# A decode block on one core: x as columns, w_o in fewer pieces, the residual matmul behind w_up, the output in one row

## The chip, the cores and the metric

The kernel runs on one core of a Trainium2 chip. The metric is the device time of one execution in microseconds (us); of several runs the median is given. Beside it stands the *span*, the time from the first to the last instruction of the kernel itself, as the hardware profiler gives it. The time is in most runs 1.8 to 2.1 us longer than the span: the trace shows semaphores being cleared after the kernel's last instruction (their last update 1.91 us after it in the trace of the kernel before).

Names: PE is the tensor engine (PEld its weight load), DVE the vector engine, ACT the scalar engine, POOL the general engine, SP the engine that issues most DMAs (SPq, ACTq: a DMA issue by SP or ACT). A DMA has *landed* when the last of its semaphore updates has come (16 for each large load).

## The reference, cut to what matters

One token goes through attention over a cache of 65536 keys and values for 8 heads of 128 columns each, four query heads per cache head, and through a gated MLP:

```
h  = x + attention(layernorm(x)) @ w_o          # x: 512 values
h2 = h + (sigmoid(n @ w_gate) * (n @ w_up)) @ w_down     # n = layernorm(h), 1792 inner columns
```

The caches have 268 MB; with the weights 282 MB must be read once. Everything else is small.

## The kernel before

All large loads are queued by SP in one order: w_q, the K and V blocks of 4 MiB each (32 of either), w_o, the last V blocks, w_gate, w_up, w_down. They go to a ring of four slots (w_o to `ktw`, the buffer of the transposed keys), and a load waits only until its place is free. The last loads are cut into pieces, so that work can begin on the first piece:

```python
WO = ((0, 16), (16, 8), (24, 4), (28, 4))          # w_o by heads: 4 pieces
WD_SPLIT = [(0, 7), (7, 12), (12, 14)]             # w_down by rows of 512
V_SPLIT = [(0, 3), (3, 4)]                         # last V block, in two pieces of two runs each
...
dma("act", lambda e: e.dma_start(x_row[:, :], A_x[0]), "x", name="x")       # one row of 512
...
for kt in range(4):                                # x into columns, by PE
    op("pe", lambda e, ...: e.matmul(ps(MISC, kt, kt + 1), lhsT=lhsT, rhs=ident[0:1, 0:1], ...), ...)
```

The tail of the program: the last heads' values, w_o, the norm, then gate, residual, up, down and the output.

```python
for i, (nm, bank) in enumerate((("wg", GB), ("wu", UB))):
    for kt in range(4):
        for c in range(4):
            op("pe", ... matmul(ps(bank, 0, FG, 32 * c, 32 * c + 1), lhsT=hc[:, kt:kt + 1], rhs=ring[...]) ...)
    if i == 0:                                     # residual h, between gate and up
        op("pe", lambda e: e.matmul(ps(YB, 0, 128), lhsT=gsel[:, :], rhs=hz[:, :], start=True, stop=False, ...), ["hz"])
op("act", ... sg = tanh(gate) ...)
op("dve", ... hh = up * sg2 ...)                   # then hhT: transpose of hh
for i, (r0, r1) in enumerate(WD_SPLIT):
    for r in range(r0, r1):
        for g in range(4):                         # four matmuls a row of w_down, on four column groups
            op("pe", ... matmul(ps(YB, 0, 128, 32 * g, 32 * g + 1), lhsT=hhT[...], rhs=wd_v[:, r, ...]) ...)
op("dve", lambda e: e.tensor_copy(y_sb[:, :], ps(YB, 0, 128)), ["y"], "ysb")
dma("sp", ... out as four rows of 128 from four partitions ...)
```

## Time and profile before

| | before |
|---|---|
| time, median of 6 runs | 661.88 us (661.62 to 662.31) |
| span of the profiled run | 659.8 us |
| read from memory | 282.3 MB, 428 GB/s over the span |
| PE, DVE, ACT busy | 64%, 53%, 6% |

The page of the profile begins with the busy time of each engine; below it the span is cut into 40 slices, with the granted TensorE clock (PEclk) and the busy share of the DMA engines in tenths:

```profile
span 659.8 us, 6128 instructions
...
PE 419.5 (64%) x2316; PEld 72.6 (11%) x1548; DVE 350.5 (53%) x446; ACT 41.8 (6%) x111; POOL 3.6 (1%) x17
...
PEclk9899687678888697776966778766878869678676
DMA  9999999999999999999999999999999999999997
...
DMA packets 11211, 282.34 MB, mean 428 GB/s; under 512 B 1225, under 2 KB 1226, under 8 KB 2250
```

The reader is to see the row of nines: the 16 DMA engines are at least 90% busy in every slice but the last, and the packets' records show no gap from 1.0 to 656.7 us. PE is busy 64% and DVE 53% of the time, and both wait for data: 160.2 of the 163.9 us that PE idles before the score matmuls end with DVE's transposed keys, and 137.4 of the 137.5 us that DVE idles before it transposes them end with a landing of K. So a microsecond saved on an engine in the middle should buy nothing; only the two ends can count, the start before the stream flows and what is left to do when it ends.

The start in the timeline (columns: start in us, duration, engine, line of the source, operation, tiles, count, and in brackets the idle time before it and what ended it):

```profile
0.80 0.51 ACTq L331 DMA_DIRECT2D x_row<-in_A_x_dram  x1
...
7.22 0.29 PE L421 MATMUL PS<-ident,x_row 1*128 1x1 bf16 x4 [7.22 <-DMA x_row<-in_A_x_dram]
...
12.69 8.78 PE L438 MATMUL PS<-ring,xz 128*8 x32
```

x arrives at 7.2 us and its norm is done before w_q has landed (12.2). The end of the timeline:

```profile
650.87 1.66 PE L816 MATMUL PS<-ring,hc 128*1 128x448 bf16 x16 [0.26 <-DVE hc L803]
...
652.46 0.80 PE L822 MATMUL PS<-hz,gsel 128*128 128x128 f32 x2
...
653.18 1.54 PE L816 MATMUL PS<-ring,hc 128*1 128x448 bf16 x16
...
654.78 0.91 DVE L828 TENSOR_TENSOR hh<-PS,sg 128x448 bf16<-128x448 f32 x1 [1.08 <-PE PS L816]
655.73 0.65 DVE L831 STREAM_TRANSPOSE hhT<-hh 128x448 bf16<-128x448 bf16 x1
...
656.43 1.05 PE L836 MATMUL PS<-ring,hhT 128*1 128x128 bf16 x56 [1.70 <-DVE hhT L831]
657.53 0.29 DVE L840 CAST y_sb<-PS 128x128 bf16<-128x128 f32 x1 [1.16 <-PE PS L836]
657.85 0.65 SPq L841 DMA_DIRECT2D out_dram<-y_sb  x1
```

L816 are gate and up, with the residual (L822) between them; L828 is hh, L831 its transpose, L836 w_down, L840 the copy of y, L841 the output. The last pieces of the chain of work that ended last (start, duration, what) are:

```profile
655.73 0.66 DVE hhT L831
...
656.43 1.08 PE PS L836 x56
...
657.53 0.29 DVE y_sb L840
```

By this view the chain is one of computing: transpose, w_down, copy. But the last piece of w_down had landed at 657.15, while the matmuls that need it began at 657.20. Chain and stream end together.

### The profile page before, as it was taken

To read this page: it belongs to the slowest core of one execution; us is meant where nothing else is said; L and a number is where in the kernel's file an instruction comes from. 1 tells how busy PE (TensorE), PEld (TensorE's weight loads), DVE (VectorE), ACT (ScalarE), POOL (GpSimd) and SP (SyncE) were. 2 spreads that over 40 slices of the span, in tenths; PEclk is the share of its full clock that TensorE was granted. 3 is DMA by queue.
4 is the path that set the end of the run, shared out by engine and by line. 5 is a ranking of instruction groups with operands and counts; after the bars stand their busy time and mean duration, and the time that the engine had idled before them with its cause. 6 is when DMAs were issued, how large, how long until landed. Compare 5 with 4: busy or idle time off the path is not lost. (4 is left out here: it accounts for less than half of the span.)

```text
span 659.8 us, 6128 instructions
## 1 busy us (share of the span) xinstructions
PE 419.5 (64%) x2316; PEld 72.6 (11%) x1548; DVE 350.5 (53%) x446; ACT 41.8 (6%) x111; POOL 3.6 (1%) x17
## 2 busy tenths in 40 slices
PE   3786587638666685566765485764856668565845
PEld 1100011001000010010100110001100101001222
DVE  3697755548436655336555374475743565553102
ACT  0100200020001100020000200002000200002000
POOL 1000000000000000000000000000000000000000
PEclk9899687678888697776966778766878869678676
DMA  9999999999999999999999999999999999999997
GB/s 397 429 445 419 439 429 429 443 417 443 425 433 441 417 445 419 439 429 429 443 417 443 429 429 441 417 445 423 435 429 429 443 419 441 429 429 419 439 418 329
DMA packets 11211, 282.34 MB, mean 428 GB/s; under 512 B 1225, under 2 KB 1226, under 8 KB 2250
## 3 DMA queue, kind: packets, MB, share of 16 engines
q1 hardware_dynamic: 11208, 282.33, 99.7%
q14 instruction: 1, 0.01, 0.0%
q10 hardware_dynamic: 2, 0.00, 0.0%
HBM read 282.33 MB, written 0.00 MB: 428 GB/s over the span
## 5 line engine op out<-in xcount | busy, mean ns | idle before, releaser
L438 PE MATMUL PS<-ktw 128*128 128x512 bf16 x1024 | 300.9, 442 | 163.9 <-DVE ktw L519 160.2
L519 DVE STREAM_TRANSPOSE ktw<-ring 128x1024 f32<-128x1024 f32 x256 | 291.7, 1206 | 137.5 <-DMA ring<-in_A_k_cache_dram 137.4
L438 PE MATMUL PS<-ring,PT_sb 128*32 x1024 | 82.8, 453 | 24.4 <-issue 16.2
L438 PEld LDWEIGHTS PS<-ktw 128*128 x256 | 27.1, 106 | 415.7 <-issue 261.5
L573 DVE STREAM_TRANSPOSE PT_sb<-P_sb 128x512 bf16<-128x512 bf16 x32 | 20.2, 684 | 53.2 <-PE PS L610 51.8
L559 ACT ACTIVATE negmax<-PS 128x1 f32<-128x1 f32 x8 | 1.4, 171 | 527.7 <-PE PS L557 527.7
L438 PEld LDWEIGHTS PS<-ring,PT_sb 128*32 x1024 | 25.3, 116 | 81.3 <-issue 76.8
L524 DVE TENSOR_REDUCE M_sb<-PS 128x1 f32<-128x512 f32 x32 | 19.9, 684 | 24.1 <-PE PS L438 24.1
L563 ACT ACTIVATE P_sb<-PS,negmax 128x512 bf16<-128x512 f32 x32 | 21.5, 685 | 0.3
L580 DVE TENSOR_REDUCE lsum<-PS 128x1 f32<-128x4 f32 x8 | 1.3, 163 | 30.5 <-PE PS L578 30.5
L550 PE MATMUL PS<-identf,gm 128*1 128x128 f32 x16 | 3.2, 286 | 16.9 <-DVE gm L548 16.9
L623 DVE TENSOR_TENSOR Lw<-O,blk_of 128x128 bf16<-128x128 bf16 x4 | 1.1, 282 | 21.7 <-ACT O L614 21.7
L607 ACT ACTIVATE po_sb<-PS,rl 128x512 bf16<-128x512 f32 x8 | 5.5, 687 | 54.4 <-PE PS L438 54.4
L438 PE MATMUL PS<-ring,xz 128*8 x32 | 8.8, 443 | 0.0
L485 DVE STREAM_TRANSPOSE qt<-qh 32x512 bf16<-32x512 bf16 x1 | 0.7, 699 | 11.9 <-ACT qh L482 11.9
L557 PE MATMUL PS<-one_f,gmrep 1*128 1x1 f32 x16 | 3.8, 306 | 5.0 <-DVE gmrep L554 5.0
L438 PE MATMUL PS<-ktw,O 128*1 x26 | 6.9, 431 | 0.0
L563 ACT ACTIVATION_READ_ACCUMULATOR P_sb<-PS,negmax 128x1 f32 x32 | 6.5, 203 | 0.0
L610 PE MATMUL PS<-sel_bf,po_sb 128*128 128x4 bf16 x32 | 2.0, 168 | 6.3 <-ACT po_sb L607 6.3
L500 ACT ACTIVATE PS<-zcol 128x512 f32<-128x512 bf16 x8 | 5.0, 622 | 0.0
L421 PE MATMUL PS<-ident,x_row 1*128 1x1 bf16 x4 | 0.3, 174 | 7.2 <-DMA x_row<-in_A_x_dram 7.2
L666 DVE TENSOR_TENSOR yr<-PS,x_row 1x512 f32<-1x512 f32 x1 | 0.7, 679 | 7.8 <-PE PS L664 7.8
(81 smaller groups left out, 69.4 us busy)
## 6 DMA issues: line engine op xcount, KB each, us to landing
ring<-in_A_k_cache_dram SPq DMA_DIRECT2D x32, 4096.0 KB, 29.6
ring<-in_A_v_cache_dram SPq DMA_DIRECT2D x31, 4096.0 KB, 27.5
ring<-in_A_wq_dram SPq DMA_DIRECT2D x1, 4096.0 KB, 12.2
ring<-in_A_v_cache_dram SPq DMA_DIRECT2D x1, 3072.0 KB, 13.1
ktw<-in_A_wo_dram SPq DMA_DIRECT2D x1, 2048.0 KB, 9.8
ring<-in_B_w_gate_dram SPq DMA_DIRECT2D x1, 1792.0 KB, 18.6
ring<-in_B_w_up_dram SPq DMA_DIRECT2D x1, 1344.0 KB, 21.2
ktw<-in_A_wo_dram SPq DMA_DIRECT2D x1, 1024.0 KB, 11.9
```

What stands on the lines that cost most here:

```text
L438: return e.add_instruction(mybir.InstMatmult(name=nc.get_next_instruction_name(), engine=mybir.EngineType.PE, ins=[rhs, lhsT], outs=[e.low ...
L500: op("act", lambda e: e.activation(ps(PO, 0, 512), bass.AP(tensor=zcol, offset=0, ap=[[1, 128], [0, 512]]), AF.Copy), ["zcol"] if h == 0 e ...
L519: op("dve", lambda e, d=dst, sr=src: e.transpose(d, sr), deps, f"T{b}.{c}", to="T")
L524: op("dve", lambda e, u=u: e.tensor_reduce(M_sb[:, u % 4:u % 4 + 1], ps(u % NS, 0, 512), AX.X, ALU.max), [f"S{b}.{NC - NR + k}"], f"mx{u}" ...
L550: op("pe", lambda e: e.matmul(ps(MISC, 0, 128, 0, 1), lhsT=gm[:, :], rhs=identf[:, :], start=True, stop=True), [f"gm{h}"], f"gmT{h}", to="Q")
L557: op("pe", lambda e: e.matmul(ps(MISC, 128, 129), lhsT=gmrep[0:1, :], rhs=one_f[0:1, 0:1], start=True, stop=True), [f"gmrep{h}"], f"neg{h}")
L559: op("act", lambda e: e.activation(negmax[:, k:k + 1], ps(MISC, 128, 129), AF.Copy, scale=-att_scale), [f"neg{h}"], f"negmax{h}")
L563: op("act", lambda e, b=b: e.activation(P_sb[:, (b % 4) * 512:(b % 4 + 1) * 512], ps(b % NS, 0, 512), AF.Exp, bias=negmax[:, k:k + 1], sca ...
L573: op("dve", lambda e, b=b: e.transpose(PT_sb[:, (b % 4) * 512:(b % 4 + 1) * 512], P_sb[:, (b % 4) * 512:(b % 4 + 1) * 512]), [f"E{b}", f"o ...
L580: op("dve", lambda e: e.tensor_reduce(lsum[:, :], ps(MISC, 132, 136), AX.X, ALU.add), [f"l{h}"], f"ls{h}", to="D")
L607: op("act", lambda e: e.activation(po_sb[:, :], ps(PO, 0, 512), AF.Copy, scale=rl[:, :]), [f"PV{NR * h + NR - 1}", f"rl{h}"], f"po{h}", to ...
L610: op("pe", lambda e, t=t: e.matmul(ps(OX, 0, 4), lhsT=po_sb[:, t * 128:(t + 1) * 128], rhs=sel_bf[:, 8 * t:8 * t + 8:2], start=(t == 0), s ...
```

## The change

Its intent is to trim the two ends: fewer and larger pieces, no transposing of x by PE, one matmul less between gate and up, one output row instead of four.

```diff
-    WO = ((0, 16), (16, 8), (24, 4), (28, 4))
-    WD_SPLIT = [(0, 7), (7, 12), (12, 14)]
+    WO = ((0, 28), (28, 4))
+    RW = 4
+    WD_SPLIT = [(0, 9), (9, 13), (13, 14)]
...
-        dma("act", lambda e: e.dma_start(x_row[:, :], A_x[0]), "x", name="x")
+        dma("act", lambda e: e.dma_start(x_col[:, :], A_x[0].rearrange("o (p k) -> (o p) k", k=4)), "x", name="x")
...      last V block: the order of K's and V's chunks changes so that each piece is one run
-                        d2, s2 = (ap.rearrange("p (h c) -> p h c", h=2)[:, :, c0 * CH:c1 * CH] for ap in (dst, src))
+                        d2, s2 = (ap[:, 2 * c0 * CH:2 * c1 * CH] for ap in (dst, src))
...      q: four transposes of x and an empty matmul go; ACT clears the sum
-        for kt in range(4):
-            lhsT = bass.AP(tensor=x_row, offset=kt, ap=[[D, 1], [4, 128]])
-            op("pe", lambda e, lhsT=lhsT, kt=kt: e.matmul(ps(MISC, kt, kt + 1), lhsT=lhsT, rhs=ident[0:1, 0:1], ...
-        ln_stats(0, ("xTp", (MISC, 0, 4)), 0, 0)
+        ln_stats(0, lambda e: e.tensor_copy(hT[0][:, :], x_col[:, :]), "x", 0, 0)
...      w_o: 28 heads are regrouped by seven small matmuls instead of three; x is added in the norm
-            op("dve", lambda e: e.tensor_tensor(yr[:, :], ps(YB, 0, D, 0, 1), x_row[:, :], ALU.add), ["yr"], "yrs")
+            op("dve", lambda e: e.tensor_copy(yr[:, :], ps(YB, 0, D, 0, 1)), ["yr"], "yrs")
...      the loop of the value matmuls computes its registers ahead of the last wait (one more branch)
-            if i == 0:
-                op("pe", lambda e: e.matmul(ps(YB, 0, 128), lhsT=gsel[:, :], rhs=hz[:, :], ...), ["hz"])
+        op("pe", lambda e: e.matmul(ps(YB, 0, 128), lhsT=gsel[:, :], rhs=hz[:, :], ...), ["hz"])
...
-        op("dve", lambda e: e.tensor_copy(y_sb[:, :], ps(YB, 0, 128)), ["y"], "ysb")
-        dma("sp", ... four rows of 128 ...)
+        for g in (0, 2, 1, 3):          # 0 and 1 by DVE, 2 and 3 by ACT, into one partition
+            ...  copy of ps(YB, 0, 128, 32 * g, 32 * g + 1) to y_sb[:, 128 * g:128 * g + 128]
+        dma("sp", lambda e: e.dma_start(out[0], y_sb[:, :]), "out", [f"ysb{g}" for g in range(4)], "out")
```

More of the change, by code (lines that the diff above doesn't have):

```diff
@@ L257, in bass_sequential_preLN__gqa_block_cached__glu_gated_glu__decode_kernel @@
         zcol = sb("zcol", [128, 1], bf16)
-        x_row = sb("x_row", [1, D], bf16)
+        x_col = sb("x_col", [128, 4], bf16)
         xz = sb("xz", [128, 4 * 16], bf16)
@@ L281, in bass_sequential_preLN__gqa_block_cached__glu_gated_glu__decode_kernel @@
         hhT = sb("hhT", [128, FG], bf16)
-        y_sb = sb("y_sb", [128, 128], bf16)
+        y_sb = sb("y_sb", [1, D], bf16)
         W0 = NKT * CH
         O3 = sb("O3", [128, NQ], bf16)
-        Lw = [sb(f"Lw{i}", [128, 128], bf16) for i in range(len(WO))]
-        row_of = {n: sb(f"row_of{n}", [128, n], bf16) for n in (16, 8, 4)}
-        blk_of = {n: sb(f"blk_of{n}", [128, 128 // n], bf16) for n in (16, 8, 4)}
+        Lw = [sb(f"Lw{i}", [128, n * DH // RW], bf16) for i, (_, n) in enumerate(WO)]
+        row_of = sb("row_of", [128, RW], bf16)
+        blk_of = sb("blk_of", [128, 128 // RW], bf16)
         head_of = sb("head_of", [128, 4], fp32)
@@ L387, in bass_sequential_preLN__gqa_block_cached__glu_gated_glu__decode_kernel, with ln_stats @@
                                           bass.AP(tensor=head_of, offset=0, ap=[[4, 128], [0, 16], [1, 4], [0, 2]])), ["head"], "lsel")
-        for n in (16, 8, 4):
-            op("dve", lambda e, n=n: e.tensor_reduce(row_of[n][:, :], identf[:, :].rearrange("p (c r) -> p r c", r=n), AX.X, ALU.max),
-               (), f"row{n}")
-            op("dve", lambda e, n=n: e.tensor_reduce(blk_of[n][:, :], identf[:, :].rearrange("p (c r) -> p c r", r=n), AX.X, ALU.max),
-               (), f"blk{n}")
+        op("dve", lambda e: e.tensor_reduce(row_of[:, :], identf[:, :].rearrange("p (c r) -> p r c", r=RW), AX.X, ALU.max), (), "row")
+        op("dve", lambda e: e.tensor_reduce(blk_of[:, :], identf[:, :].rearrange("p (c r) -> p c r", r=RW), AX.X, ALU.max), (), "blk")
         op("dve", lambda e: e.tensor_reduce(bass.AP(tensor=gsel, offset=0, ap=[[128, 128], [32, 4]]),
                                             identf[:, :].rearrange("p (s j) -> p s j", s=4), AX.X, ALU.add), ["gs0", "identf"], "gsel")
-        def ln_stats(i, src_dep, bank, c0):
-            op("dve", lambda e: e.tensor_copy(hT[i][:, :], ps(*src_dep[1])), [src_dep[0]], f"hT.{i}")
+        def ln_stats(i, fill, dep, bank, c0):
+            op("dve", fill, [dep], f"hT.{i}")
             op("dve", lambda e: e.tensor_tensor(sq[:, :], hT[i][:, :], hT[i][:, :], ALU.mult), [f"hT.{i}"], f"sq.{i}")
@@ L416, in ln_rstd @@
                f"rstd.{i}")
-        for kt in range(4):
-            lhsT = bass.AP(tensor=x_row, offset=kt, ap=[[D, 1], [4, 128]])
-            op("pe", lambda e, lhsT=lhsT, kt=kt: e.matmul(ps(MISC, kt, kt + 1), lhsT=lhsT, rhs=ident[0:1, 0:1], start=True, stop=True,
-                                                          skip_group_check=True),
-               ["x", "ident"] if kt == 0 else (), "xTp" if kt == 3 else None)
-        ln_stats(0, ("xTp", (MISC, 0, 4)), 0, 0)
+        ln_stats(0, lambda e: e.tensor_copy(hT[0][:, :], x_col[:, :]), "x", 0, 0)
         ln_rstd(0, 0, 0, 1.0)
@@ L461, in project_q @@
         def project_q(e):
-            def none(start, stop):
-                return e.matmul(ps(1, 0, 512, 0, 8), lhsT=qz[:, 0:8], rhs=qz[:, 0:512], start=start, stop=stop, skip_group_check=True)
-            none(True, False)
             e.reg_mov(reg(e, 0), addr_of(xz, 8 + 7))
@@ L478, in project_q @@
                     e.reg_alu(reg(e, 4 + kt), reg(e, 4 + kt), 1024, ALU.add)
-            return none(False, True)
-        op("pe", project_q, ["xz", "wq", "identf", "lsel", "onef", "sel", "gsel", "row4", "PTz", "qz0"], "q")
+            return e.matmul(ps(1, 0, 512, 0, 8), lhsT=qz[:, 0:8], rhs=qz[:, 0:512], start=False, stop=True, skip_group_check=True)
+        op("act", lambda e: e.activation(ps(1, 0, 512, 0, 8), bass.AP(tensor=zcol, offset=0, ap=[[1, 8], [0, 512]]), AF.Copy), ["zcol"], "zq")
+        op("pe", project_q, ["zq", "xz", "wq", "identf", "lsel", "onef", "sel", "gsel", "row", "PTz", "qz0"], "q")
         op("act", lambda e: e.activation(
@@ L513, in dve_block @@
                 n = b * NC + c
-                src = ring[:, s * SLOT + c * CH: s * SLOT + (c + 1) * CH].bitcast(fp32)
+                at = s * SLOT + (2 * (c % NR) + c // NR) * CH
+                src = ring[:, at:at + CH].bitcast(fp32)
                 dst = ktw[:, (n % NKT) * CH:(n % NKT + 1) * CH].bitcast(fp32)
@@ L588, in pv_regs @@
                         e.reg_alu(reg(e, i), R["p"], 2 * (128 * tq + half), ALU.add)
-                        e.reg_alu(reg(e, i + 4), R["v"], 2 * (half * NR * TC + 4 * tq) * 128, ALU.add)
+                        e.reg_alu(reg(e, i + 4), R["v"], 2 * (half * TC + 4 * tq) * 128, ALU.add)
         def pv(b):
@@ L616, in head_out @@
                 clear_out(h + 1)
-        YT, STB, GB, UB, YB, OT = 0, MISC, 2, 3, 5, (1, 2, 3, 1)
+        YT, STB, GB, UB, YB, OT = 0, MISC, 2, 3, 5, (1, 1)
         def regroup(i):
             j0, n = WO[i]
+            m = 128 // RW
             op("dve", lambda e: e.tensor_tensor(Lw[i][:, :].rearrange("p (j c) -> p j c", j=n),
-                                                bass.AP(tensor=O2, offset=j0, ap=[[NQ, 128], [1, n], [0, 128 // n]]),
-                                                bass.AP(tensor=blk_of[n], offset=0, ap=[[128 // n, 128], [0, n], [1, 128 // n]]), ALU.mult),
-               [f"o2.{(j0 + n) // GS - 1}", f"blk{n}"], f"Lw{i}")
-            op("pe", lambda e: e.matmul(ps(OT[i], 0, n), lhsT=Lw[i][:, :], rhs=row_of[n][:, :], start=True, stop=True),
-               [f"Lw{i}", f"PT{NB - 1}" if i == 0 else None], f"O3p{i}")
+                                                bass.AP(tensor=O2, offset=j0, ap=[[NQ, 128], [1, n], [0, m]]),
+                                                bass.AP(tensor=blk_of, offset=0, ap=[[m, 128], [0, n], [1, m]]), ALU.mult),
+               [f"o2.{(j0 + n) // GS - 1}", "blk"], f"Lw{i}")
+            for v in range(n // RW):
+                lhsT = bass.AP(tensor=Lw[i], offset=v, ap=[[n * m, 128], [n // RW, 128]])
+                op("pe", lambda e, v=v, lhsT=lhsT: e.matmul(ps(OT[i], RW * v, RW * v + RW), lhsT=lhsT, rhs=row_of[:, :], start=True,
+                                                            stop=True, skip_group_check=True),
+                   [f"Lw{i}", f"PT{NB - 1}" if i == 0 else None] if v == 0 else (), f"O3p{i}" if v == n // RW - 1 else None)
             op("dve", lambda e: e.tensor_copy(O3[:, j0:j0 + n], ps(OT[i], 0, n)), [f"O3p{i}"], f"O3.{i}")
@@ L640, in project7 @@
         def project7():
-            for i in range(3):
-                regroup(i)
-            waits = [d for i in range(3) for d in (f"O3.{i}", f"wo{i}")]
+            regroup(0)
+            waits = ["O3.0", "wo0"]
             def rows(e):
@@ L723, in pe_flow @@
             pv_regs(e)
+            goto("products", "sums")
             section("B")
             e.reg_alu(p, p, 2 * 512, ALU.add)
-            e.reg_alu(v, v, 2 * CH, ALU.add)
+            e.reg_alu(v, v, 2 * 2 * CH, ALU.add)
             e.reg_alu(m, m, -1, ALU.add)
@@ L731, in rest @@
             def rest():
-                section("VL")
+                pv_regs(e)
                 e.reg_mov(m, 1)
                 e.reg_mov(k, 0)
-            away("br_ne", k, 0, "rest", rest, "sums")
+                section("VL")
+            away("br_ne", k, 0, "rest", rest, "products")
             away("br_eq", w, w0 - 12, "outs", lambda: section("O"))
@@ L797, in bass_sequential_preLN__gqa_block_cached__glu_gated_glu__decode_kernel @@
         P.part = {}
-        regroup(3)
-        project(range(NQ - GS, NQ), O3, ["O3.3", "wo3"], last=True)
-        ln_stats(1, ("yT", (YT, 0, 4)), STB, 0)
+        regroup(1)
+        project(range(NQ - GS, NQ), O3, ["O3.1", "wo1"], last=True)
+        ln_stats(1, lambda e: e.tensor_tensor(hT[1][:, :], ps(YT, 0, 4), x_col[:, :], ALU.add), "yT", STB, 0)
         op("dve", lambda e: e.scalar_tensor_tensor(hc[:, :], ps(STB, 0, 1).to_broadcast([128, 4]), -1.0 / D, hT[1][:, :],
@@ L820, in bass_sequential_preLN__gqa_block_cached__glu_gated_glu__decode_kernel @@
                        ["hc"] * (kt == 0 and c == 0) + dep, f"gu{i}" if kt == 3 and c == 3 else None)
-            if i == 0:
-                op("pe", lambda e: e.matmul(ps(YB, 0, 128), lhsT=gsel[:, :], rhs=hz[:, :], start=True, stop=False, skip_group_check=True),
-                   ["hz"])
+        op("pe", lambda e: e.matmul(ps(YB, 0, 128), lhsT=gsel[:, :], rhs=hz[:, :], start=True, stop=False, skip_group_check=True), ["hz"])
         op("act", lambda e: e.activation(sg[:, :], ps(GB, 0, FG), AF.Tanh, scale=rstd[1][:, 0:1]), ["gu0", "rstd.1"], "sg")
@@ L839, in bass_sequential_preLN__gqa_block_cached__glu_gated_glu__decode_kernel @@
                        ["hhT", f"wd{i}"] if r == r0 and g == 0 else (), "y" if last else None)
-        op("dve", lambda e: e.tensor_copy(y_sb[:, :], ps(YB, 0, 128)), ["y"], "ysb")
-        dma("sp", lambda e: e.dma_start(out[0].rearrange("o (g n) -> (o g) n", g=4),
-                                        bass.AP(tensor=y_sb, offset=0, ap=[[32 * 128, 4], [1, 128]])), "out", ["ysb"], "out")
+        for g in (0, 2, 1, 3):
+            if g < 2:
+                op("dve", lambda e, g=g: e.tensor_copy(y_sb[:, 128 * g:128 * g + 128], ps(YB, 0, 128, 32 * g, 32 * g + 1)), ["y"], f"ysb{g}")
+            else:
+                op("act", lambda e, g=g: e.activation(y_sb[:, 128 * g:128 * g + 128], ps(YB, 0, 128, 32 * g, 32 * g + 1), AF.Copy),
+                   ["y"], f"ysb{g}")
+        dma("sp", lambda e: e.dma_start(out[0], y_sb[:, :]), "out", [f"ysb{g}" for g in range(4)], "out")
         P.at_end = ("out",)
```

## The prediction

> **What bounds it now.** The DMA stream. In the page's slices the 16 DMA engines are 9 tenths busy or more in 39 of 40; 282.34 MB move in a span of 659.8 us. In the trace's packets data flows without a gap from 1.0 to 656.7 us, one 4 MiB block landing every 9.71 us (432 GB/s). [...] PE is busy 64%, DVE 53%; loads are issued a median 28 to 30 us before they land, so a few us on PE, DVE or ACT in the middle are free.
>
> Only two ends count. (a) The tail: the last V piece lands at 644.1, and the chain of waits runs PV, head output, w_o, norm, gate, up, hh, transpose to the w_down matmuls at 656.43. (b) The stream: the last w_down piece lands at 657.15, just before its matmuls (about 657.3). They are tied within 0.2 us. Then y copy 0.29, output DMA issued 657.85, landed 659.5, end 659.8.
>
> **What the change does.**
> - Larger packets. Rates of the last loads, from landings, by bytes per partition: 32 KB 432 GB/s, 16 KB 428, 12 KB 425, 8 KB 421, 4 KB 410. w_o as one 28 KB row: 8.67 us becomes about 8.5. Last V block in 24 and 8 KB rows instead of 12 and 4: 9.95 becomes about 9.8. w_down 7/5/2 to 9/4/1: neutral. The stream ends about 0.3 us earlier (estimate).
> - x as 128 rows of 8 B instead of one of 1024 B. [...] no trace here shows the cost of 8 B. I allow 0.1 to 0.4 us of stream, eating that gain. x may land later than 7.2; q is needed only about 18 us later than now: harmless.
> - Start: four transposing matmuls and an empty one go (under 1 us), off the path.
> - Steady state: one more branch per PV block, hidden.
> - w_o regroup: one DVE product of 896 columns (about 1.1 us, estimate), seven small matmuls instead of three rounds: about 1 us earlier at 617, off the path.
> - Residual matmul behind w_up: 0.72 us leave the chain; hh and transpose end near 655.6. But w_down pieces land at about 654.9 to 657, so PE waits for DMA: only about 0.2 us shows.
> - Output: four copies in two pairs (DVE, ACT) instead of one: +0.15 to 0.2 us (estimate). One row instead of four: issue perhaps 0.1 us shorter (x, one row, took 0.51; out, four rows, 0.65).
> - Last w_down piece has 4 matmuls instead of 8 after it: -0.1 us.
>
> **Time.** Summed, -0.1 to -0.4 us of 662.05: I predict 661.75 us, range 661.0 to 662.5. Faster by over 2% 0.01, within 2% 0.98, slower by over 2% 0.01.
>
> **What would show it.** Blocks still land every 9.71 us; packets without a gap to about 656.4 to 656.7; PE idle before the w_down matmuls, released by DMA and no longer by the transpose; up matmuls directly behind gate, hh 0.7 us earlier; y copies ending about 0.45 us after the last matmul.
>
> **What would make it wrong.** The 8 B rows interleave with w_q packets so badly that q comes over 18 us late and the queue runs dry; [...] the tail runs at a lower granted clock than now (about 0.55 from 645 to 655), so PE ends last[...].

0.3 us less for the larger packets, 0.1 to 0.4 more for x, 0.2 less for the residual, 0.15 to 0.2 more for the copies, 0.1 less for the issue and 0.1 less for the last piece come to 0.1 to 0.45 us less, put as 0.1 to 0.4. The terms for x and for the copies are estimates; the runs gave about 0.14 and 0.31. The product of 896 columns took 1.07 us. The 18 us of slack for q are an estimate that was not tested, as q came 5.8 us later; the added branch was not timed alone, but the K and V blocks landed a median 9.71 us apart before and after.

## More of the kernel before

The title that the change came with also says "TensorE at 438 instructions". Nothing in the diff tells why anyone would count them.

## The result, and the profile after

| | before | changed |
|---|---|---|
| time, median of 6 runs | 661.88 us (661.62 to 662.31) | 661.39 us (661.26 to 661.46) |
| span of the profiled run | 659.8 us | 659.5 us |

The ratio is 0.9992 (95% interval 0.9979 to 1.0005). Such a ratio is the mean time of one kernel's fast runs over the mean of the other's of the same rounds, so it is not quite the ratio of the medians above. All six runs of the changed kernel lie below all six of the kernel before, yet the interval still contains 1.

The page and the start of the timeline of the changed kernel:

```profile
span 659.5 us, 6120 instructions
...
DMA  9999999999999999999999999999999999999997
```

```profile
0.81 0.38 ACTq L332 DMA_DIRECT2D x_col<-in_A_x_dram  x1
...
14.96 0.17 DVE L417 CAST hT<-x_col 128x4 f32<-128x4 bf16 x1 [10.79 <-DMA x_col<-in_A_x_dram]
...
18.48 8.36 PE L431 MATMUL PS<-ring,xz 128*8 x32 [2.31 <-issue]
```

The nines stay. x, now 128 rows of 8 B, was issued at the same time as before and lands at 14.9 instead of 7.2: the trace has its packets in groups of 16 between 5.2 and 13.4 us, about 1.2 us apart (two of the eight came together), and their semaphore updates in one more group at 13.9 to 14.6. So the q projection starts at 18.5 instead of 12.7. The K loads behind it were queued far ahead (a median 29.1 us from issue to landing): no slice of the DMA row shows it. The end:

```profile
650.65 3.16 PE L813 MATMUL PS<-ring,hc 128*1 128x448 bf16 x32 [0.25 <-DVE hc L800]
...
653.74 0.80 PE L818 MATMUL PS<-hz,gsel 128*128 128x128 f32 x2
653.86 0.92 DVE L823 TENSOR_TENSOR hh<-PS,sg 128x448 bf16<-128x448 f32 x1 [0.37 <-PE PS L813]
654.81 0.65 DVE L826 STREAM_TRANSPOSE hhT<-hh 128x448 bf16<-128x448 bf16 x1
...
655.60 1.88 PE L831 MATMUL PS<-ring,hhT 128*1 128x128 bf16 x56 [1.07 <-DMA ring<-in_B_w_down_dram]
656.78 0.41 PEld L831 LDWEIGHTS PS<-ring,hhT 128*1 128x1 bf16 x20 [0.34 <-DMA ring<-in_B_w_down_dram]
657.53 0.57 ACT L839 ACTIVATE y_sb<-PS 1x128 bf16<-1x128 f32 x2 [4.53 <-PE PS L831]
657.53 0.59 DVE L837 CAST y_sb<-PS 1x128 bf16<-1x128 f32 x2 [2.08 <-PE PS L831]
658.19 0.33 SPq L841 DMA_DIRECT2D out_dram<-y_sb  x1
```

```profile
631.19 25.54 DMA ring<-in_B_w_down_dram
656.73 0.04 issue
656.78 0.73 PE PS L831 x19
```

Line by line: gate and up are now one group (L813), the residual (L818) runs beside hh (L823), and hh starts 0.92 us earlier than before (653.86 against 654.78); 0.22 of it is there already when gate begins (650.65 against 650.87), and the residual's place gives the other 0.70. The w_down matmuls (L831) start at 655.60, stop, and go on at 656.78, released by a DMA. The chain of work that ended last no longer runs through the transpose: it hangs on the load of w_down. The last matmul ends at 657.48, at the same time as before. Behind it the y copies now end at 658.13 instead of 657.82, but the output's DMA takes less: from its issue to the end of the span 1.36 us (658.19 to 659.55) instead of 1.90 (657.85 to 659.75).

Landings of the last loads, in us (start of the w_o load is the landing before it):

```
                        before     changed
block before w_o        604.77     605.01
w_o, first 28 heads     613.44     613.55    8.67 -> 8.54
block before last V     634.15     634.22
last V block, whole     644.10     644.03    9.95 -> 9.80
w_up, whole             652.75     652.66
w_down, last piece      657.15     657.04    4.40 -> 4.38
```

The stream ended 0.11 us earlier, and the larger rows gave what was expected of them (0.13 and 0.15 us). In this one pair of traces, then, the gain is made behind the last matmul. But the two had unlike clocks at the end: from 656 to 657 us TensorE was granted 1.00 of its clock before and 0.50 after. The experiments show that one pair of traces was not enough.

### The profile page after: what moved, and what is told of

It reads as the page before. It is cut to its first block, busy times and chain, and to the rows that moved or that the text cites. A ratio compares the mean times of both kernels' runs of the same rounds, so it can differ in the third digit from the quotient of the medians.

```text
span 659.5 us, 6120 instructions
## 1 busy us (share of the span) xinstructions
PE 418.8 (64%) x2315; PEld 73.5 (11%) x1547; DVE 349.8 (53%) x439; ACT 43.0 (7%) x114; POOL 3.6 (1%) x17
## 5 line engine op out<-in xcount | busy, mean ns | idle before, releaser
L616 DVE TENSOR_TENSOR Lw<-O,blk_of 128x896 bf16<-128x896 bf16 (+1 forms) x2 | 1.4, 681 | 20.7 <-ACT O L606 20.7
## 6 DMA issues: line engine op xcount, KB each, us to landing
ring<-in_A_k_cache_dram SPq DMA_DIRECT2D x32, 4096.0 KB, 29.1
```

The source lines that it names most:

```text
L616: op("dve", lambda e: e.tensor_tensor(Lw[i][:, :].rearrange("p (j c) -> p j c", j=n), bass.AP(tensor=O2, offset=j0, ap=[[NQ, 128], [1, n], ...
```

## The experiments

Twelve kernels were run, four in each of three calls, each call on another chip. All outputs are right. "Before" in the table are the runs of the kernel before on the same chip; the spans tell more than the times.

| run | median time | before | ratio (95%) | median span | before |
|---|---|---|---|---|---|
| e1_x_row | 664.62 | 662.07 | 1.0039 (1.0026 to 1.0053) | 659.6 | 660.1 |
| e2_out_four | 661.54 | 662.07 | 0.9993 (0.9979 to 1.0007) | 659.7 | 660.1 |
| e3_x_four_times | 662.33 | 662.07 | 1.0003 (0.9990 to 1.0017) | 660.5 | 660.1 |
| e4_resid_between | 662.00 | 662.07 | 1.0002 (0.9988 to 1.0015) | 660.1 | 660.1 |
| c_after | 661.51 | 662.31 | 0.9990 (0.9977 to 1.0002) | 659.5 | 660.0 |
| e5_out_only | 663.10 | 662.31 | 1.0012 (0.9999 to 1.0026) | 660.7 | 660.0 |
| e6_wo_four | 663.46 | 662.31 | 1.0013 (1.0000 to 1.0026) | 661.2 | 660.0 |
| e8_pad | 664.13 | 662.31 | 1.0018 (1.0002 to 1.0034) | 659.4 | 660.0 |
| c_before | 662.08 | 662.29 | 1.0000 (0.9986 to 1.0014) | 660.1 | 660.3 |
| e12_resid_only | 661.83 | 662.29 | 0.9999 (0.9985 to 1.0012) | 659.9 | 660.3 |
| e11_out_79 | 662.03 | 662.29 | 0.9996 (0.9983 to 1.0010) | 660.0 | 660.3 |
| b1_best | 661.24 | 662.29 | 0.9986 (0.9972 to 0.9999) | 659.3 | 660.3 |

The ratios of most of these kernels are not clear of noise. In the spans the whole change is: 11 runs of the changed kernel took 659.3 to 659.7 us, 34 runs of the kernel before beside the experiments 659.6 to 660.6. Differences of 0.2 us between two rows of different chips are at the edge of what can be told.

My theory when they began: what the packets give, x's small rows take, and the gain is that of the output. Rivals: the gain comes from the stream; or from the residual matmul's place in the chain.

### e1_x_row: x as one row again

```diff
-            x_col: 128 rows of 8 B;  hT[0] = copy of x_col
+            x_row: one row of 1024 B, four transposing matmuls, hT[0] = copy of their sums
```

> The changed kernel with x loaded as one row of 1024 B again and four transposing matmuls. If the 128 rows of 8 B cost the DMA stream time that nothing returns (my theory): w_q lands about 0.3 us earlier (12.2 instead of 12.5), every later landing about 0.2 us earlier, the last w_down landing 656.8 instead of 657.04, and the time is 0.2 us less, about 661.2. If the rows are filled into gaps of the stream and cost latency only (rival): the q projection starts at 12 instead of 18.5, all later landings stay within 0.05 us, the time stays at 661.4.

x landed at about 7 and q began with w_q, as expected. The stream: the block before w_o landed, by the first of its updates, at 604.17 to 604.28 in all seven traces that load x as a row (mean 604.21), and at 604.19 to 604.45 in the six of the changed kernel's kind (mean 604.35). So 128 rows of 8 B cost the stream about 0.14 us by these means, not 0.2; the two groups overlap, and each mixes chips. By the measure that was set beforehand the theory missed: the last w_down piece landed at 657.03 instead of 656.8, as in the changed kernel (657.04), and the median span is not below the changed kernel's (659.6 against 659.5). The time rose to 664.6, by 3.2 us against the changed kernel, and neither theory has that. The span did not rise (659.3 to 659.6): the 3.2 us lie behind the last instruction.

There the trace shows the semaphores being cleared, in five groups, of 47 to 51 by their numbers. The start of each group, counted from the end of the span, with the last update of all:

```
                PE instructions   207-255  156-206  105-155  54-104   7-53    last
before                447            0.66     0.77     0.82    0.83    0.99    1.91
changed               448            0.76     0.88     0.93    0.94    1.09    2.01
e6_wo_four            449            0.66     0.78     0.82    0.83    1.15    2.06
e8_pad                456            0.66     0.78     0.82    0.83    4.67    5.59
e1_x_row              457            0.66     0.77     0.82    0.83    4.43    5.35
```

The instructions are counted in the built program, a bf16 matmul as two (load and multiply), an fp32 matmul as four (in the trace of the kernel before, too, the one residual matmul, fp32, is two loads and two multiplies). A recount over all blocks of the program gives 27 more in each of the five (474, 475, 476, 483, 484), so only the differences are to be relied on. One group comes more than 3 us late, and the four transposes with their wait had made PE's program nine longer.

### e8_pad: four unused matmuls

```diff
+        for kt in range(4):
+            op("pe", ... matmul(ps(MISC, 256 + kt, 257 + kt), lhsT=ident[:, :], rhs=ident[:, 0:1], ...))
```

> The changed kernel with four unused matmuls on PE at the start, while it idles: the PE program grows from 448 to 456 instructions by my count, everything else stays. The first run (457 instructions) was 3.2 us slower though its span was not: in its trace one engine's clearing of semaphores behind the program came 3.1 us late. If that comes from the length of the PE program: time about 3.2 us above the changed kernel, 664.6, span unchanged at 659.5. If it came from loading x as a row: no change, 661.4.

These matmuls run at the start, while PE waits for x, and nobody reads them. The span stayed (659.3 to 659.7), and time minus span became 5.5, 2.4, 2.4, 5.5, 5.2 and 4.4 us in its six runs, against 1.8 to 2.9 for the changed kernel. So the longer PE program is the cause (its length, or the place of what it moves; the run does not part the two), and e1 was not slow because of x. It is not all or nothing: two of six runs escaped with 2.4. This may be why someone counted instructions; the title's 438 is not reproduced by either count. What happens in those 3 us is not shown. The trace of the changed kernel, a fast run of 661.46 us, has a packet of 16,384 B with the kind "instruction" 0.99 us behind the span too, so such a packet alone does not tell.

### e2_out_four: the output as before

```diff
-        four copies on DVE and ACT into one partition; one row to memory
+        one copy on DVE; four rows to memory
```

> The changed kernel with the output written as four rows from one copy again. My theory, that the gain of the whole change was made behind the last matmul: from the last matmul's end to the end of the span 2.3 us instead of 2.0, so about 0.25 us slower, 661.65. Rival, that the gain came from the stream and its larger packets and that four copies against one and one row against four cancel: within 0.05 us of the changed kernel.

```profile
656.78 0.52 PE L831 MATMUL PS<-ring,hhT 128*1 128x128 bf16 x20 [0.41 <-DMA ring<-in_B_w_down_dram]
```

From the end of the last matmul to the end of the span: 2.27 us (657.29 to 659.56), and 2.07 in the changed kernel (657.48 to 659.55). Both traces of the kernel before have 2.27 too. So one row is worth 0.2 us, nearly what I expected. (The last matmul ends 0.19 us earlier here than in the changed kernel because the clock was 1.00: the last 20 matmuls took 0.52 us, there about 0.7.) Yet the time was only 0.15 us above the changed kernel's, and the medians of spans differ by 0.2 (659.7 against 659.5, on different chips). The output is a part of the gain and not the whole.

### e3_x_four_times: the cost of 8 B rows, times four

```diff
+        x_more = [sb(f"x_more{i}", [128, 4], bf16) for i in range(3)]
+        for i in range(3):
+            dma("act", ... dma_start(x_more[i][:, :], A_x[0].rearrange("o (p k) -> (o p) k", k=4)), f"xm{i}", ...)
```

> The changed kernel with the 8 B load of x issued four times (three copies are not used). If each such load takes about 0.2 us from the stream: last landing about 0.6 us later, near 657.6, time about 662.0. If it costs latency only: the time stays at 661.4 and the last landing at 657.0.

The last piece landed at 658.03, 0.99 us later than in the changed kernel, so 0.33 us for each further load; the median span was 1.0 us above c_after's. The cost on the stream is real: such a load is not latency alone. The run does not part the size of the rows from the number of loads; three further loads with one long row each were not tried. Why a further load costs more than the first (0.14) is open.

### e4_resid_between: the residual matmul back between gate and up

```diff
-        op("pe", ... matmul(ps(YB, 0, 128), lhsT=gsel[:, :], rhs=hz[:, :], ...), ["hz"])      # behind up
+            if i == 0:
+                op("pe", ... the same, between gate and up ...)
```

> The changed kernel with the residual matmul back between gate and up. My theory: hh and the transpose end 0.7 us later, about 656.2, still before the second w_down piece lands at 656.7, so the time changes by 0 to 0.1 us. Rival, that the chain of PE, ACT and DVE bounds the end: 0.5 to 0.7 us slower, about 662.0.

My theory missed here. The median span was 660.1, that of the kernel before, 0.6 us above c_after (on another chip). The stream ended as ever (657.02), but the w_down matmuls started at 656.05 and ran to 657.72: 1.66 us for 56 matmuls, where the first trace of the kernel before had shown 1.05. The granted clock was 0.50. In this trace PE, not the DMA, ended last:

```profile
656.05 1.66 PE L832 MATMUL PS<-ring,hhT 128*1 128x128 bf16 x56 [1.70 <-DVE hhT L827]
```

### c_before: the kernel before

> The kernel before itself, as a control with a second profile. Earlier traces show the TensorE clock granted in slots of 3.4 us at 0.5 or 1.0 whose place differs from run to run. In the first trace of this kernel the 56 w_down matmuls fell into a slot of 1.0 (55 ns a row of four). If the slot matters: in a trace where they fall into 0.5 (107 ns a row) the last matmul ends near 658.2 instead of 657.5 and the span is near 660.4 instead of 659.8; spans of its runs scatter over 659.8 to 660.5. If not, all spans are within 0.2 us.

The same microsecond near the end, first in the first trace of the kernel before, then in the second. Columns: window, length, busy time and count on PE, PEld, DVE, ACT and POOL, then the granted clock, the DMA share and GB/s:

```profile
656.00:657.00 1.00, 0.57 (x44) 0.57 (x48) 0.37 (x1) 0.00 (x0) 0.00 (x0) 1.00 0.40 148
```

```profile
656.00:657.00 1.00, 0.97 (x40) 0.97 (x44) 0.00 (x0) 0.00 (x0) 0.00 (x0) 0.50 0.34 127
```

The clock was 1.00 in one and 0.50 in the other. The timeline of the second:

```profile
656.03 1.66 PE L836 MATMUL PS<-ring,hhT 128*1 128x128 bf16 x56 [1.69 <-DVE hhT L831]
657.74 0.29 DVE L840 CAST y_sb<-PS 128x128 bf16<-128x128 f32 x1 [1.77 <-PE PS L836]
658.06 0.66 SPq L841 DMA_DIRECT2D out_dram<-y_sb  x1
```

The transpose came 0.40 us earlier than in the first trace, and yet the copy started 0.21 us later: at half the clock a row of four w_down matmuls takes 107 ns instead of 55. The spans of the kernel before ran from 659.6 to 660.6 (14 runs). But for the last record of a trace, the clock records are 0.5 or 1.0 in stretches that are multiples of 3.41 us, and their edges lie elsewhere in every run (the last two at 654.5 and 657.9 us in the first trace of the kernel before, at 645.8 and 649.2 in that of the changed kernel). What sets the state is not shown here. The expected 660.4 for this trace came out as 660.0, since the transpose had been earlier. Only two runs of this kernel have a trace, so that the clock makes most of the scatter of 1.0 us is argued, not shown.

### e12_resid_only: the move of the residual matmul alone

> The kernel before with only the residual matmul moved behind w_up. The fourth run (the changed kernel with it moved back) had median span 660.1, as the kernel before, against 659.5 of the changed kernel. So the new theory: this move is most of the gain, because the w_down matmuls start 0.7 us earlier and are behind the DMA also where the clock is 0.5: span 659.6 to 659.7, time about 0.4 us below the kernel before. The theory of the prediction, 0.2 us at most: span 659.9.

The edit is that of e4 the other way round, made to the kernel before. The end of the timeline:

```profile
655.32 0.91 PE L834 MATMUL PS<-ring,hhT 128*1 128x128 bf16 x28 [0.97 <-DVE hhT L829]
...
656.61 0.99 PE L834 MATMUL PS<-ring,hhT 128*1 128x128 bf16 x28 [0.37 <-DMA ring<-in_B_w_down_dram]
...
657.65 0.29 DVE L838 CAST y_sb<-PS 128x128 bf16<-128x128 f32 x1 [2.39 <-PE PS L834]
```

At the same half clock as in c_before, w_down starts 0.71 us earlier, does half of its matmuls and waits for the second piece. Median span 659.9 (659.8 to 660.0), against 660.2 for the 14 runs of the kernel before. So the move alone is worth about 0.3 us by the medians of the spans, 0.24 by their means; the times are not clear of noise (0.9985 to 1.0012). The expectation of 659.6 to 659.7 was too good; the prediction's 0.2 is a little less, but this run does not refute it.

The traces show how: it puts PE ahead, so that the clock decides over less. From the last landing to the end of the last matmul it took 0.61 us in c_before and 0.43 here, both at clock 0.50. The clock still counts: in the changed kernel the same stretch took 0.44 us at clock 0.50 and 0.27 in e2 at 1.00. That the move takes away the slow half of the spread fits the five spans here, but is argued from them.

### c_after: the changed kernel, a control

> The changed kernel itself once more, as a control on this chip beside the others: about 0.5 us below the kernel before.

Median span 659.5 against 660.0, and 0.80 us in the times. Times on this chip are noisier: time minus span has a second value near 2.9 in some runs of either kernel.

### e5_out_only: the output's change alone

> The kernel before with only the output changed (four copies on two engines, one row to memory). The second run's trace put the gain of this part at 0.17 us (2.24 us from the last matmul's end to the span's end with four rows, 2.07 with one). If that is right and it is the lesser part: 0.15 to 0.2 us below the kernel before. If the output made the whole gain: 0.5 us below.

It got worse: median span 660.7 against 660.0. Two things add to this in the trace: a stop of SP, and a last w_down piece that landed at 657.45, where the other four traces with these pieces of w_down have 657.08 to 657.17; why is open. The last copy of y ended at 658.42, and the DMA was issued at 658.89:

```profile
657.83 0.59 DVE L842 CAST y_sb<-PS 1x128 bf16<-1x128 f32 x2 [1.41 <-PE PS L836]
658.89 0.33 SPq L846 DMA_DIRECT2D out_dram<-y_sb  x1
```

SP had ended its first wait at 658.43 and then stood still for 0.45 us. The same stop is in every trace, but elsewhere: in the changed kernel it comes *behind* the output's DMA (658.52 to 658.99), where SP would wait for the landing anyway. With a wait more in SP's program (the output now waits for two engines), the DMA had become the 81st instruction instead of the 80th. In the changed kernel the w_o pieces that were merged bring it to the 79th. (A recount of the built programs gives the same numbers.)

### e11_out_79: the same, with one DMA less ahead of it

```diff
-        W_SPLIT = {"wg": [(0, 4)], "wu": [(0, 3), (3, 4)]}
+        W_SPLIT = {"wg": [(0, 4)], "wu": [(0, 4)]}
```

> The kernel before with the output changed to one row (as in e5) and w_up loaded in one piece instead of two, so that SyncE's program has one DMA less ahead of the output. In e5 and e6 SyncE stopped 0.45 us between its wait and the output's DMA; in all others the same stop lies behind that DMA. If it belongs to a fixed place in SyncE's program (between the 80th and 81st instruction by my count): here the DMA is issued 0.07 us after the wait, the stop comes behind it, and the span is 0.5 us below e5's, about 0.2 us below the kernel before. If the stop came from the output itself: 0.45 us before the DMA again.

```profile
657.87 0.59 DVE L842 CAST y_sb<-PS 1x128 bf16<-1x128 f32 x2 [1.77 <-PE PS L836]
658.53 0.33 SPq L846 DMA_DIRECT2D out_dram<-y_sb  x1
```

y ended at 658.46, the DMA was issued at 658.53, and the stop (658.86 to 659.30) came behind it. Median span 660.0 against 660.2 for the kernel before: the 0.2 us of one row (w_up in one piece is in this too). So the stop belongs to a place in SP's program and not to the output. It does not always stand behind the 80th instruction: in the changed kernel it comes behind the 79th, in e2 behind the 78th. In the built programs a branch to the last instructions follows the output's DMA. The stop comes at that branch in every trace but those of e5 and e6; there the branch is the 82nd instruction, and the stop has come already between the 80th and the 81st. What happens in it is not shown. Two parts of the change that look unrelated, fewer pieces of w_o and the output in one row, belong together: without the first, the second costs more than it gives.

### e6_wo_four: w_o in four pieces again

```diff
-    WO = ((0, 28), (28, 4))
+    WO = ((0, 16), (16, 8), (24, 4), (28, 4))
```

> The changed kernel with w_o loaded in four pieces (16, 8, 4, 4 KB per partition) as before, and regrouped in four. If larger rows gave back what x's 8 B rows take: w_o's last landing and all later ones 0.1 to 0.15 us later, last landing near 657.15, time 0.1 to 0.15 us above the changed kernel. If row size does not matter: equal. Its PE program is one instruction longer (449 by my count against 448)[...].

The four pieces took 9.95 us from the block before to the last landing, where two took 9.80 in the control (by the first update of each landing): 0.15 us, as expected. But the span rose by 1.7 us, for two other reasons. One is SP's stop before the output (y at 659.29, issued at 659.73). The other is in the timeline earlier, at the row of w_o (L660 is its last matmul) and the values behind it:

```profile
627.95 0.38 PE L660 MATMUL PS<-ktw,O 128*1 128x512 bf16 x1
...
629.73 0.63 PE L431 MATMUL PS<-ring,PT_sb 128*32 x8 [1.40 <-PEq L169]
...
632.79 0.80 SPq L362 DMA_DIRECT2D ring<-in_A_v_cache_dram  x2
...
634.87 1.40 PE L431 MATMUL PS<-ring,PT_sb 128*32 x16 [2.11 <-PEq L169]
```

The row of w_o itself ended 2.3 us later than in the changed kernel (its last matmul began at 627.95 against 625.61): three rounds of regrouping took 2.26 us up to its first matmul, where the one round took 0.81. Then PE stood still 1.40 us between w_o and the next values, went through them with further gaps, and freed the slot for the last V block only at 632.79 (628.44 in the changed kernel). The block before landed at 634.27, so the load was issued 1.5 us ahead of the end of the queue. That was too late: the stream carried 236 and 215 KB in the two microseconds from 633 where it carries 431 elsewhere, and the last V block landed 1.1 us late. The 1.40 us are put down to PE's sequencer. Why it stops there in this program and not in the changed one is open; the run does not measure the pieces of w_o alone.

### b1_best: a version with what was learned

```diff
     changed kernel, with x as a row (as in e1), the x column taken from hT[0], and
-        yr = sb("yr", [1, 512], fp32)
+        yr = sb("yr", [1, 512], bf16)               # its four transposing matmuls: bf16 instead of fp32
-    WD_SPLIT = [(0, 9), (9, 13), (13, 14)]
+    WD_SPLIT = [(0, 9), (9, 11), (11, 13), (13, 14)]
```

> An attempt at a better kernel: the changed one with x as one row of 1024 B, the w_o row held in bf16 and transposed by bf16 matmuls (PE program 449 instructions, below the 456 that cost 3 us), and w_down in 9, 2, 2 and 1 rows (output DMA at the same place in SyncE's program as in the kernel before). Column matmuls 0.4 instead of 2.0 us, stream 0.1 us earlier, at most 0.1 us less behind the last landing: 0.1 to 0.3 us below the changed kernel. If the end is bound by the DMA landing alone and x's rows cost nothing: equal.

```profile
655.26 1.85 PE L836 MATMUL PS<-ring,hhT 128*1 128x128 bf16 x56 [1.38 <-DMA ring<-in_B_w_down_dram]
...
656.84 0.09 PEld L836 LDWEIGHTS PS<-ring,hhT 128*1 128x1 bf16 x4 [0.20 <-DMA ring<-in_B_w_down_dram]
...
657.17 0.59 DVE L842 CAST y_sb<-PS 1x128 bf16<-1x128 f32 x2 [2.37 <-PE PS L836]
657.82 0.33 SPq L846 DMA_DIRECT2D out_dram<-y_sb  x1
```

PE's program has 449 instructions and the output's DMA is SP's 80th; neither penalty appeared. The four transposes took 0.29 us instead of 2.02, the stream ended at 656.79, the last matmul at 657.11. Median time 661.24, median span 659.3. It is the one kernel of twelve whose interval against the kernel before stays below 1, and only just (0.9972 to 0.9999). Against the changed kernel the gain is 0.2 us by c_after's median span, as expected, but next to nothing by that of the changed kernel's first six runs (about 659.4); it is not clear of noise.

## Why the prediction was right or wrong

The predicted time, 661.75 us in a range of 661.0 to 662.5, held: 661.39 was measured. "Within 2%" held as well. Neither says much: the range is 1.5 us wide and the whole effect 0.5. The forecast gain itself, 0.1 to 0.4 us from 662.05 (the median of the first three runs), was too small: from median to median, 661.88 to 661.39, it is 0.49. The reading beneath it, that the DMA stream bounds the kernel and only its two ends can count, was right: the DMA row is all nines but for the last slice in both pages. Point by point:

- **Larger packets, about 0.3 us.** Right: 0.13 us at w_o, 0.15 at the last V block, w_down neutral (4.40 against 4.38).
- **x as 8 B rows, 0.1 to 0.4 us of stream, late x harmless.** In the range: about 0.14 us by the means of overlapping groups of traces, x at 14.9, no DMA slice lost. Stream in sum 0.11 us earlier.
- **w_o regroup, "about 1 us earlier at 617".** The regrouping did shrink, from 1.95 us to 0.81 up to the row's first matmul, but it began 1.24 us later in this trace, so the row was not earlier (617.77 against 617.67). Off the path, as said.
- **"only about 0.2 us shows" of the residual matmul.** The mechanism was right (hh 0.9 us earlier; the last w_down matmuls wait for the DMA, while for the first piece transpose and DMA are tied, and in c_after the transpose came last), the size was rather too small. Alone it brought 0.24 to 0.3 us (e12); taken back out of the changed kernel it cost about 0.6 (e4, across chips). I had read the duration of w_down, 1.05 us, from a single trace in which the clock happened to be 1.0; at 0.5 it is 1.66, and then PE, not the DMA, was the last. The prediction had named just this, a lower clock in the tail, among what would make it wrong, but had left it out of the sum.
- **Output: +0.15 to 0.2 us for the copies, perhaps 0.1 us less for the issue.** Both terms were mis-sized, and the sign of their sum was wrong. The copies cost 0.31 us more (each 0.28, in two rounds), the issue took 0.33 instead of 0.65, and from issue to the end of the span 1.36 instead of 1.90. In sum the row is worth 0.2 us.
- **Last w_down piece with 4 matmuls: -0.1 us.** Not seen: the last matmul ended at 657.48 in both traces, because the second piece now has four rows, lands at 656.73, and is worked off at half the clock. At like clocks it shows no more: e12 with its eight matmuls ended 0.43 us behind the last landing, the changed kernel with four 0.44, both at 0.50.
- **What would make it wrong.** A cost of PE's layout was named, but as a stall inside the tail. The runs showed a cost behind the span (e1, e8), a stop on SP that costs where it comes before the output (e5, e6), and one stall of PE near the end (1.40 us in e6, cause open). The change itself pays for none of them; they come into sight only when a part of it is undone or made alone.

Added up from the runs, one row of output gives 0.2 us, the residual's move about 0.25, the stream's earlier end 0.1: about the 0.5 that were measured. Why it is not more: the stream carried the same 282 MB, and its blocks landed every 9.71 us (432 GB/s) in both kernels; what was had were fractions at the end.

## What to carry to other kernels

When a kernel runs at the rate of its DMA stream, ask only what is left to do when the last byte lands, and start that part early enough that the clock decides over little of it, instead of reading its length from one trace (the last 56 matmuls here took 1.05 us at clock 1.00 in one run and 1.66 at 0.50 in another of the same kernel). The place of an instruction in its engine's program had a price here that no diff shows (0.45 us on SP in e5, 2.6 us behind the span in e8): undo parts one at a time, compare the time with the span, and look at where each stop falls, since an edit that loses alone (e5) can gain beside another.
